# Re-spacing the DFT pieces of a spectral mixing and MLP kernel between its MLP steps

## The chip, the cores and the metric

The kernel runs on one core of a Trainium2 chip. The metric is the device time of one launch in microseconds (us); a time is the median of several launches. Every launch compared here counts as fast, that is, none was over 1.5% above the fastest launch of the same kernel.

TensorE (PE) does the matmuls and writes them to PSUM. VectorE (DVE) and ScalarE (ACT) move results out of PSUM. SyncE (SP) issues most DMAs. GpSimd (POOL) issues the loads of filters, weights and `x`; those of `x` change it from float32 to float16 on the way.

## The reference, cut to what matters

```python
B, S, C, DFF = 8, 3008, 256, 2048
X = np.fft.rfft(x, axis=1)                       # x: (8, 3008, 256)
y = np.fft.irfft(X * (filt_r + 1j * filt_i), n=S, axis=1)
h = y.reshape(B * S, C) @ w_in                   # (24064, 2048)
s = np.sin(alpha * h)
out = (h + s * s / (alpha + 1e-9)) @ w_out       # (24064, 256)
```

## The kernel before

The two transforms of a batch are split by 3008 = 47 x 64 into three stages. Between the stages the data goes through DRAM, because each stage needs another dimension on the partitions.

- Stage 1 (matmuls `pa`) turns `x` tiles into `t1` tiles, which are stored to the DRAM tensor `d1` ("the d1 store", `d<-t` in the profile). The whole of `d1` is read back as eight `t2` transfers (`t<-d`).
- Stage 2 (`pb`, then a product with the filter on VectorE, then `pc`) turns `t2` into `g`, stored to `d2` (`d<-g`). `d2` is read back as four `t4` tiles (also `t<-d`).
- The last stage (`pd`) turns `t4` into `y`, the input of the MLP.

The MLP (`ph` hidden, `po` projection) is one stream of 49 chunks of 8 steps, 48 steps to a batch on average. Stage pieces of the following batches are put in between, each at a step that a plan gives. The parts that matter (cuts marked `# ...`):

```python
xpool = pool("xp", 4)                   # four x tiles: one batch
fps = pool("fps", 2, PSUM)              # two PSUM buffers for pa, pb, pc, pd

def load_x(b):                          # four loads on GpSimd's queue
    for ch in range(4):
        xt = xpool.tile([NR, 8, C], FP16, name=f"x_{b}_{ch}", tag="x")
        ins = nc.gpsimd.dma_start(out=xt, in_=...)
        if b == 1:
            after(ins, marks["t4"])     # a true wait on a landing
        # ...

def stage1(u):
    ch, half = divmod(u, 2)
    if u == 0:
        st["x"] = load_x(b)
    # ... two pa matmuls from x tile ch, evicted to t1; with half == 1:
    #     nc.sync.dma_start(out=d1_rows[...], in_=st["t1"])
    # ... with u == 7: the eight t2 loads, each waiting for all of d1

def stage2(u):
    # ... with u < 12: pb, xf = copy(pb), two products; with u > 0: pc of u - 1, eviction to g

plan = {1: [-45 + i for i in range(8)],
        2: [-29 + 14 * i / 13 for i in range(13)],
        3: [-10, -9] + [-7 + 2 * i for i in range(14)]}
# ... a piece of batch b stands at step 48 * b + plan[stage][i];
#     batch 1 has 8 + i for stage 1 and 23 + i for stage 2

for k in range(len(chunks) + 1):
    for j in range(8):                  # one step
        hidden(k, 2 * j); hidden(k, 2 * j + 1)
        while pending and pending[0][0] <= step:
            pending.pop(0)[2]()         # the stage pieces due
        # ... project(k - 1, ...)
        step += 1
```

`behind(a, b)` orders two instructions at build time; `after(a, b)` makes `a` wait for `b` at run time. Anything else waits only for its data and its buffers.

## Time and profile before

| | before |
|---|---|
| time, median of the first 3 launches | 840.69 us (840.57 to 841.27) |
| span of the profiled launch | 837.2 us, granted TensorE clock 0.988 |
| first hidden matmul | 54.3 us |
| stalls of TensorE over 60 ns, all / after 80 us | 48.1 / 12.9 us |
| last stage-1 matmul to first stage-2 matmul, batches 2 to 7 | 16.7 us |

The head of the page: busy microseconds, and their share of the span, for each engine.

```profile
span 837.2 us, 16122 instructions
...
PE 799.8 (96%) x5793; PEld 544.2 (65%) x5793; DVE 628.1 (75%) x1119; ACT 613.0 (73%) x1200; POOL 28.3 (3%) x55
```

PE is busy 96% of the span. A busy record does not show a full rate, so the fourth table row comes from the start times of the single matmuls in the trace: the floor of a matmul with N columns is N / 2.4 GHz plus 2.5 ns (the Trainium skill's figure that the prediction names), and what lies above it, to the next matmul's start, is its stall. (The few float32 matmuls at the start are charged four times N; the trace has 853 ns for one with N = 512.) Back to back the trace shows 109 ns for N = 256 and 216 ns for N = 512, which is that floor.

The waits view of TensorE: who waited for whom, microseconds in total, times, longest.

```profile
PE pd L219 <- DMA t<-d: 10.9, 2, 9.3
PE pa L157 <- DMA x<-in_x_dram: 6.3, 1, 6.3
PE po L369 <- DVE w L337: 2.6, 1, 2.6
PE pb L180 <- DMA t<-d: 1.5, 1, 1.5
```

Nearly all of this is the start.

The timeline around the end of batch 2's stage 1: start, duration (microseconds), engine, line, operation, out<-in, count. A DMA line shows its issue, not its transfer. The transfer's end shows in who waits for it: all eight t2 loads wait for the last d1 store.

```profile
175.84 0.52 POOL L118 DMA_DIRECT2D x<-in_x_dram  x1 [4.21 <-PE pa L157]
...
177.53 4.81 SPq L161 DMA_DIRECT2D d<-t  x2
...
179.68 0.60 PE L157 MATMUL pa<-x,wf_t 94*96 94x512 f16 x2
...
180.57 0.52 POOL L118 DMA_DIRECT2D x<-in_x_dram  x1 [4.22 <-PE pa L157]
...
187.89 5.32 SPq L169 DMA_DIRECT2D t<-d  x8
...
196.60 0.38 PE L180 MATMUL pb<-t,d_t 128*128 128x256 f16 x2
```

Read it from top to bottom. Each x load of batch 3 goes out when a stage-1 matmul of batch 2 lets go of its buffer, so x loads and d1 stores run side by side. The last d1 store, issued at 182.0 us by the trace, lands at 187.8; the t2 loads follow at once. The first pair lands at 192.1 and is needed at 196.6: there are 4.5 us to spare. Not every batch has so much: batch 3's pair lands 1.8 us before its `pb`, batch 5's 2.2 us.

One more place, the timeline inside batch 2's dense stage 2:

```profile
201.89 0.75 DVE L187 TENSOR_TENSOR p<-xf,filt 128x512 f16<-128x512 f16 x2
...
202.56 0.68 DVE L137 CAST g<-pc 128x512 f16<-128x512 f32 x1
...
202.90 0.38 PE L369 MATMUL po<-w,v 128*128 128x256 f16 x2
...
203.30 0.60 PE L199 MATMUL pc<-p,e_t 128*128 128x256 f16 x4
```

The second `po` starts at 203.01, and `pc` could start 0.11 us later. It starts at 203.30, just after VectorE's eviction of the `pc` before it ended (202.56 + 0.68 = 203.24) and gave back one of the two `fps` buffers. After 80 us there are 24 such stalls before `pc`, 4.6 us.

### The profile page before, as it was taken

What the parts mean: (1) busy time and instruction counts of PE and PEld (TensorE: products, weight loads), DVE (VectorE), ACT (ScalarE), POOL (GpSimd) and SP (SyncE); (2) the same over time, 40 slices, a digit from 0 to 9 for tenths busy, and PEclk for the clock granted to TensorE, in tenths of its full rate; (3) what the DMA queues carried; (4) which work ended last, traced back from release to release, by engine and by line L of the source; (5) the groups of instructions that cost most, each with busy time, mean ns of one, the idle gap of its engine ahead of it and who ended that gap; (6) DMA issues with size and microseconds to landing.
All of it is one profiled execution on the core that took longest, in us unless ns stands there. A gap on an engine that the chain in (4) does not pass through costs nothing.

```text
span 837.2 us, 16122 instructions
## 1 busy us (share of the span) xinstructions
PE 799.8 (96%) x5793; PEld 544.2 (65%) x5793; DVE 628.1 (75%) x1119; ACT 613.0 (73%) x1200; POOL 28.3 (3%) x55
## 2 busy tenths in 40 slices
PE   5758999999999999999999999999999999999996
PEld 2425676667776677666776677666777677666674
DVE  3658886778877788777877788777877778777772
ACT  4536886787868787787877777777877878677763
POOL 3210000000000000000000000000000000000000
PEclk9969999999999999999999999999999999999999
DMA  9985835185344744266242763447443353421111
GB/s 220 218 255 117 200 89 130 51 174 116 82 135 81 171 99 109 75 141 153 65 130 60 165 137 82 115 91 171 92 96 94 97 113 83 115 58 38 38 40 45
DMA packets 93495, 94.98 MB, mean 113 GB/s; under 512 B 8084, under 2 KB 82852, under 8 KB 93416
## 3 DMA queue, kind: packets, MB, share of 16 engines
q1 hardware_dynamic: 84784, 75.02, 34.5%
q0 software_dynamic: 6704, 18.09, 12.5%
q10 hardware_dynamic: 1928, 0.86, 0.5%
q8 instruction: 45, 0.74, 0.3%
q14 instruction: 34, 0.28, 0.1%
HBM read 58.02 MB, written 49.81 MB: 129 GB/s over the span
## 4 chain that ended last, share of the span: by engine, by line
PE 83%; DMA 7%; ACT 4%; issue 3%; DVE 2%; POOL 0%; SPq 0%; ACTq 0%; DVEq 0%; POOLq 0%
PE po L369 36%; PE ph L354 35%; PE pc L199 4%; PE pa L157 3%; ACT cos L357 2%; PE pd L219 2%; PE pb L180 2%; DMA t<-d 1%; DMA w_out<-in_moe_w_out_dram 1%; DMA d<-g 1%; DMA d_t<-d_tbl 1%; DVE p L187 1%; DMA x<-in_x_dram 1%; DMA filt<-in_filt_i_dram 1%; ACT t L135 1%
## 5 line engine op out<-in xcount | busy, mean ns | idle before, releaser
L358 DVE SCALAR_TENSOR_TENSOR v<-cos,ph 128x512 f16<-128x512 f32 (+1 forms) x768 | 484.0, 672 | 164.0 <-ACT cos L357 163.5
L357 ACT ACTIVATE cos<-ph 128x512 f32<-128x512 f32 (+1 forms) x768 | 411.6, 589 | 153.9 <-PE ph L354 152.5
L369 PE MATMUL po<-w,v 128*128 128x256 f16 x3008 | 400.9, 273 | 2.6 <-DVE w L337 2.6
L354 PE MATMUL ph<-y,w 128*128 128x512 f16 (+1 forms) x1536 | 391.5, 377 | 0.2 <-ACT y L135 0.2
L369 PEld LDWEIGHTS <-v 128*128 128x128 f16 x3008 | 289.0, 98 | 80.9 <-issue 8.7
L354 PEld LDWEIGHTS <-w 128*128 128x128 f16 x1536 | 150.4, 98 | 101.0 <-issue 4.6
L187 DVE TENSOR_TENSOR p<-xf,filt 128x512 f16<-128x512 f16 x192 | 72.1, 419 | 4.9 <-ACT xf L183 4.5
L375 ACT COPY o<-po 128x512 f32<-128x512 f32 x96 | 55.6, 579 | 17.7 <-PE po L369 15.5
L135 ACT CAST t<-pa 96x512 f16<-96x512 f32 x89 | 51.0, 589 | 19.0 <-PE pa L157 18.9
L183 ACT CAST xf<-pb 128x512 f16<-128x512 f32 x96 | 57.0, 595 | 8.1 <-PE pb L180 5.5
L219 PEld LDWEIGHTS <-t 96*128 96x128 f16 x512 | 36.3, 100 | 39.8 <-DMA t<-d 11.8
L199 PE MATMUL pc<-p,e_t 128*128 128x256 f16 x384 | 59.7, 275 | 2.6 <-DVE p L187 1.5
L157 PE MATMUL pa<-x,wf_t 94*96 94x512 f16 x128 | 47.2, 408 | 10.1 <-DMA x<-in_x_dram 6.3
L219 PE MATMUL pd<-wi_t,t 96*128 96x94 f16 x512 | 43.4, 208 | 11.1 <-DMA t<-d 10.9
L135 ACT CAST y<-pd 128x376 f16<-128x376 f32 x82 | 39.1, 479 | 12.5 <-PE pd L219 12.5
L199 PEld LDWEIGHTS <-e_t 128*128 128x128 f16 x384 | 37.6, 99 | 15.6 <-issue 7.1
L180 PE MATMUL pb<-t,d_t 128*128 128x256 f16 x192 | 38.2, 283 | 2.5 <-DMA t<-d 1.5
L135 ACT CAST g<-pc 128x512 f16<-128x512 f32 x64 | 38.7, 605 | 1.6 <-PE pc L199 1.6
L137 DVE CAST t<-pa 96x512 f16<-96x512 f32 x39 | 26.6, 683 | 15.8 <-PE pa L157 15.8
L180 PEld LDWEIGHTS <-d_t 128*128 128x128 f16 x192 | 18.9, 101 | 23.8 <-issue 4.6
L118 POOL DMA_DIRECT2D x<-in_x_dram x32 | 16.7, 524 | 502.8 <-PE pa L157 490.5
L157 PEld LDWEIGHTS <-wf_t 94*96 94x96 f16 x128 | 16.6, 129 | 19.6 <-issue 9.9
(28 smaller groups left out, 94.3 us busy)
## 6 DMA issues: line engine op xcount, KB each, us to landing
d<-t SPq DMA_DIRECT2D x32, 384.0 KB
d<-g SPq DMA_DIRECT2D x64, 192.0 KB
t<-d SPq DMA_DIRECT2D x32, 384.0 KB
x<-in_x_dram POOLq DMA_DIRECT2D x32, 376.0 KB, 6.9
t<-d SPq DMA_DIRECT2D x60, 192.0 KB
out_dram<-o SPq DMA_DIRECT2D x72, 94.0 KB
w_in<-in_moe_w_in_dram POOLq DMA_DIRECT2D x2, 1024.0 KB, 9.2
w_out<-in_moe_w_out_dram POOLq DMA_DIRECT2D x1, 2048.0 KB, 11.6
```

The lines of the kernel that those rows point to most:

```text
L135: marks["act"] = nc.scalar.copy(out=dst, in_=src)
L157: marks["pe"] = nc.tensor.matmul(out=ps[0:NK, :], lhsT=wf_t, rhs=st["x"][ch][:, n0:n0 + 2, :], start=True, stop=True)
L180: nc.tensor.matmul(out=ps[:, i, :], lhsT=d_t[:, s, :], rhs=st["t2"][s // 6][:, s % 6, :], start=True, stop=True)
L183: nc.scalar.copy(out=xf, in_=ps)
L187: marks["prod", u] = nc.vector.tensor_tensor(out=pt, in0=xf, in1=f_t[k][:, 2 * u:2 * u + 2, :], op=ALU.mult)
L199: nc.tensor.matmul(out=ps[:, i, :], lhsT=e_t[:, k, 2 * w + i, :], rhs=pr[k][:, i, :], start=(k == 0), stop=(k == 1))
L219: nc.tensor.matmul(out=psv[:, i, :], lhsT=st["t4"][:, 4 * half + i, cb * 128:cb * 128 + 128], rhs=wi_t, start=True, stop=True)
L354: nc.tensor.matmul(out=ps[:, 0:n], lhsT=w1[:, cb, jb * 128:jb * 128 + 128], rhs=y_cols[:, cb, c0:c0 + n], start=(cb == 0), stop=(cb == 1))
L357: nc.scalar.activation(out=cs[:, 0:n], in_=ps[:, 0:n], func=AFT.Sin, bias=float(np.pi / 2))
L358: marks["snake"] = nc.vector.scalar_tensor_tensor(out=v[k][:, jb, 0:n], in0=cs[:, 0:n], scalar=-1.0, in1=ps[:, 0:n], op0=ALU.add, op1=ALU. ...
L369: nc.tensor.matmul(out=pso[k][:, t % 2, :], lhsT=v[k][:, jb, 128 * t:128 * t + 128], rhs=w2[:, jb, :], start=(jb == 0), stop=(jb == 15))
L375: nc.scalar.copy(out=o[:, 0:nb, :], in_=pso[k][:, 0:nb, :])
```

## The change

The intent: spread stage 2 over 24 steps so that evictions keep up, move the last stage further into its own batch's MLP, put the x loads behind the t2 loads, and load each t4 tile one ahead. Stage 1 moves from -45 to -50, stage 2 from -29 to -36, and odd batches go four steps earlier still. That cuts the room between the last stage-1 piece and the first stage-2 piece from nine steps to seven. The core of the diff, long refactorings cut:

```diff
         def stage1(u):
-            if u == 0:
+            if u == 0 and b < 2:
                 st["x"] = load_x(b)
# ... stage2 is split into forward, product and inverse, same work
+        def load_t4(ch):
+            st["t4", ch] = t4pool.tile([NK, 8, C], FP16, name=f"t4_{b}_{ch}", tag="t4")
+            marks["t4"] = nc.sync.dma_start(out=st["t4", ch], in_=d2_rows[:, 8 * ch:8 * ch + 8, :])
         def stage3(u):
             if rest == 0:
-                # ... load t4 tile ch
+                for c in ([0, 1] if ch == 0 else [ch + 1] if ch < 3 else []):
+                    load_t4(c)
# ...
+        if b >= 2:
+            pieces.append((0, lambda: st.update(x=load_x(b))))
# ... the sign of the imaginary part moves from e_t to the filter tile
-    plan = {1: [-45 + i for i in range(8)],
-            2: [-29 + 14 * i / 13 for i in range(13)],
-            3: [-10, -9] + [-7 + 2 * i for i in range(14)]}
+    def at_step(b, stage, i):
+        if b == 1 and stage < 3:
+            return 6 + i if stage == 1 else 21 + i
+        return 48 * b - 4 * (b % 2) + (-72 if stage == 0 else -50 + i if stage == 1
+                                       else -36 + 24 * i / 12 if stage == 2
+                                       else -6 + i if i < 4 else -1 + 2 * (i - 4))
```

A side effect: `w_out`'s load waits for `marks["t4"]`, the last t4 load emitted so far. That was tile 0 of batch 0 and is now tile 1.

More of the change, by code (lines that the diff above doesn't have):

```diff
@@ L171, in stage1, with forward @@
                     st["t2"].append(t2)
+        def forward(u):
+            ps = (ops if b == 0 else fps).tile([128, 2, C], FP32, name=f"pb_{b}_{u}",
+                                               tag="o" if b == 0 else "f")
+            for i in range(2):
+                s = 2 * u + i
+                nc.tensor.matmul(out=ps[:, i, :], lhsT=d_t[:, s, :],
+                                 rhs=st["t2"][s // 6][:, s % 6, :], start=True, stop=True)
+            xf = xfpool.tile([128, 2, C], FP16, name=f"xf_{b}_{u}", tag="xf")
+            nc.scalar.copy(out=xf, in_=ps)
+            st["xf", u] = xf
@@ new lines, in product, with inverse @@
+        def product(k, u):
+            pt = ppool.tile([128, 2, C], FP16, name=f"p_{b}_{u}_{k}", tag="p")
+            marks["prod", u] = nc.vector.tensor_tensor(out=pt, in0=st["xf", u],
+                                                       in1=f_t[k][:, 2 * u:2 * u + 2, :], op=ALU.mult)
+            return pt
+        def inverse(w):
+            pr = st.pop(("p", w))
+            if w % 3 == 0:
+                st["g"] = gpool.tile([128, 6, C], FP16, name=f"g_{b}_{w}", tag="g")
+            ps = fps.tile([128, 2, C], FP32, name=f"pc_{b}_{w}", tag="f")
+            for i in range(2):
+                for k, pt in enumerate(pr):
+                    nc.tensor.matmul(out=ps[:, i, :], lhsT=e_t[:, k, 2 * w + i, :],
+                                     rhs=pt[:, i, :], start=(k == 0), stop=(k == len(pr) - 1))
+            i0 = 2 * (w % 3)
+            evac(st["g"][:, i0:i0 + 2, :], ps, i0 != 2 if b == 0 else None)
+            if w % 3 == 2:
+                for p in range(2):
+                    a0 = p * NS + 6 * (w // 3)
+                    nc.sync.dma_start(out=d2[a0:a0 + 6, :, :].rearrange("s n c -> n s c"),
+                                      in_=st["g"][64 * p:64 * p + 64, :, :])
@@ L173, in stage2 @@
         def stage2(u):
             if u < 12:
-                ps = (ops if b == 0 else fps).tile([128, 2, C], FP32, name=f"pb_{b}_{u}",
-                                                   tag="o" if b == 0 else "f")
-                for i in range(2):
-                    s = 2 * u + i
-                    nc.tensor.matmul(out=ps[:, i, :], lhsT=d_t[:, s, :],
-                                     rhs=st["t2"][s // 6][:, s % 6, :], start=True, stop=True)
-                xf = xfpool.tile([128, 2, C], FP16, name=f"xf_{b}_{u}", tag="xf")
@@ L183, in stage2 @@
-                nc.scalar.copy(out=xf, in_=ps)
-                pr = []
-                for k in range(2):
-                    pt = ppool.tile([128, 2, C], FP16, name=f"p_{b}_{u}_{k}", tag="p")
-                    marks["prod", u] = nc.vector.tensor_tensor(out=pt, in0=xf, in1=f_t[k][:, 2 * u:2 * u + 2, :],
-                                                               op=ALU.mult)
-                    pr.append(pt)
-                st["p", u] = pr
-            if u > 0:
-                w = u - 1
-                pr = st.pop(("p", w))
-                if w % 3 == 0:
-                    st["g"] = gpool.tile([128, 6, C], FP16, name=f"g_{b}_{w}", tag="g")
-                ps = fps.tile([128, 2, C], FP32, name=f"pc_{b}_{w}", tag="f")
-                for i in range(2):
-                    for k in range(2):
-                        nc.tensor.matmul(out=ps[:, i, :], lhsT=e_t[:, k, 2 * w + i, :],
-                                         rhs=pr[k][:, i, :], start=(k == 0), stop=(k == 1))
-                i0 = 2 * (w % 3)
-                evac(st["g"][:, i0:i0 + 2, :], ps, i0 != 2 if b == 0 else None)
-                if w % 3 == 2:
-                    for p in range(2):
-                        a0 = p * NS + 6 * (w // 3)
-                        nc.sync.dma_start(out=d2[a0:a0 + 6, :, :].rearrange("s n c -> n s c"),
-                                          in_=st["g"][64 * p:64 * p + 64, :, :])
@@ L209, in stage3 @@
+                forward(u)
+                st["p", u] = [product(k, u) for k in range(2)]
+            if u > 0:
+                inverse(u - 1)
+        def load_t4(ch):
+            st["t4", ch] = t4pool.tile([NK, 8, C], FP16, name=f"t4_{b}_{ch}", tag="t4")
+            marks["t4"] = nc.sync.dma_start(out=st["t4", ch], in_=d2_rows[:, 8 * ch:8 * ch + 8, :])
         def stage3(u):
@@ L212, in stage3 @@
             if rest == 0:
-                t4 = t4pool.tile([NK, 8, C], FP16, name=f"t4_{b}_{ch}", tag="t4")
-                marks["t4"] = nc.sync.dma_start(out=t4, in_=d2_rows[:, 8 * ch:8 * ch + 8, :])
-                st["t4"] = t4
+                for c in ([0, 1] if ch == 0 else [ch + 1] if ch < 3 else []):
+                    load_t4(c)
             ps = fps.tile([128, 4, 128], FP32, name=f"pd_{b}_{u}", tag="f")
@@ L219, in stage3 @@
                 nc.tensor.matmul(out=psv[:, i, :],
-                                 lhsT=st["t4"][:, 4 * half + i, cb * 128:cb * 128 + 128],
+                                 lhsT=st["t4", ch][:, 4 * half + i, cb * 128:cb * 128 + 128],
                                  rhs=wi_t, start=True, stop=True)
@@ L266, in dup_filter @@
         gs = slice(6 * g, 6 * g + 6)
-        for k in range(2):
-            ins = nc.vector.tensor_copy(out=f_t[k][64:128, gs, :], in_=f_t[k][0:64, gs, :])
+        for ins in (nc.vector.tensor_copy(out=f_t[0][64:128, gs, :], in_=f_t[0][0:64, gs, :]),
+                    nc.vector.tensor_scalar(out=f_t[1][0:64, gs, :], in0=f_t[1][64:128, gs, :],
+                                            scalar1=-1.0, scalar2=None, op0=ALU.mult)):
             behind(ins, marks["prod", 3 * g - 2] if g else s1_dve)
@@ L275 @@
                 ins = nc.gpsimd.dma_start(
-                    out=f_t[k][32 * q:32 * q + 32, 6 * g:6 * g + 6, :],
+                    out=f_t[k][64 * k + 32 * q:64 * k + 32 * q + 32, 6 * g:6 * g + 6, :],
                     in_=bass.AP(tensor=filt.tensor, offset=filt.offset + off,
@@ L287 @@
         behind(nc.scalar.mul(e_t[:, 0, gs, :], pse, 0.125), s1_act)
-        nc.vector.tensor_copy(out=e_t[0:64, 1, gs, :], in_=e_t[64:128, 0, gs, :])
-        nc.vector.tensor_scalar(out=e_t[64:128, 1, gs, :], in0=e_t[0:64, 0, gs, :],
-                                scalar1=-1.0, scalar2=None, op0=ALU.mult)
+        for p in range(2):
+            nc.vector.tensor_scalar(out=e_t[64 * p:64 * p + 64, 1, gs, :],
+                                    in0=e_t[64 - 64 * p:128 - 64 * p, 0, gs, :],
+                                    scalar1=-1.0, scalar2=None, op0=ALU.mult)
     ones = cpool.tile([128, 128], FP32)
@@ L391, in store @@
             p += cnt
-    plan = {1: [-45 + i for i in range(8)],
-            2: [-29 + 14 * i / 13 for i in range(13)],
-            3: [-10, -9] + [-7 + 2 * i for i in range(14)]}
+    def at_step(b, stage, i):
[4 more added lines that the diff above has]
+                                       else -6 + i if i < 4 else -1 + 2 * (i - 4))
     pending = [(1 + i % 4 + 8 * (i // 4), 0, piece) for i, (_, piece) in enumerate(first[25:])]
     for b in range(1, B):
-        at = {1: 0, 2: 0, 3: 0}
+        at = {0: 0, 1: 0, 2: 0, 3: 0}
         for stage, piece in spectral(b):
-            at_step = 48 * b + plan[stage][at[stage]]
-            if b == 1 and stage < 3:
-                at_step = 8 + at[stage] if stage == 1 else 23 + at[stage]
+            pending.append((at_step(b, stage, at[stage]), b, piece))
             at[stage] += 1
-            pending.append((at_step, b, piece))
     pending.sort(key=lambda p: p[0])
```

## The prediction

> **What bounds the kernel now.** TensorE. The page gives PE 799.8 us of a 837.2 us span (96%), and the windows view 19.8 to 20.0 of nearly every 20 us from 80 us on. That proves little (the Trainium skill, "Perfetto Trace Analysis", opening note, calls matmul busy time a bad metric because matmuls are pipelined), so I took start-to-start times from the trace. Back to back, 128x256 projections start every 109 ns, 128x512 hidden matmuls every 216 ns. That agrees with the skill's "TensorE: Matmul & The Clock Gate", section "Wait — 56ns, not 53.3ns?": N / 2.4 GHz plus about 2.5 ns. Charging each matmul that floor, the matmuls after 80 us need 735 us and lose only 13 us to stalls over 60 ns. By what came after the stall: stage 1 (pa) 5.8 us in 29 stalls, the second stage's inverse (pc) 4.6 us in 24, the last stage (pd) 2.0 us, of which 1.78 us is one wait at 141 us for batch 1's t4. The remaining loss is the start: first hidden matmul at 54.3 us, and 2.65 us of waiting for w_out at 62 us. So at most 13 us, 1.5%, can be won.
>
> **What the change does.** Matmuls, evictions and bytes stay. The filter's sign moves from e_t to f_t: 421 ns against 423 ns, nothing.
> - Stage 2 over 24 steps rather than 14. The timeline at 200 to 214 us shows the stall: pc waits for one of two fps buffers, whose eviction (683 ns) stands on VectorE behind other work; about four 0.18 to 0.24 us stalls a batch. With a piece every second step VectorE has about 4.2 us for what it now does in 2.45. Gone: -4 us.
> - Batch 1 moves two steps earlier while its last stage stays at step 38: the 1.78 us wait goes: -1.8 us.
> - Stage 1 still fills both fps buffers, now with more last-stage pieces in the same steps for odd batches: +0.5 us.
> - From the last stage-1 matmul to the first stage-2 matmul, room falls from 9 steps (16.7 us: 179.9 to 196.6) to 7, about 13 us. The first t2 pair lands 11.3 to 15 us after that matmul (x loads run beside the d1 stores, which take 5 to 9 us). Stage 1's own matmuls release the x loads (the waits view), so they should not move. Batches 3 and 5 may wait 1.5 to 2 us each, some others less: +2 us. If the x loads do move behind the t2 loads: 0.
> - w_out's load now waits for t4 tile 1 rather than 0, starting 1 to 1.5 us later, where PE already waits: +1 us.
> - Room between stage 2 and the last stage stays six steps; t4 lands within 0.8 us of need: 0 to +1 us.
>
> **Sum.** 840.7 - 5.8 + 3.5 = about 838.4; the t2 waits are uncertain, so lower: 837.5 us, 8 in 10 between 833 and 841.5. Faster by over 2%: 0.01; within 2%: 0.98; slower by over 2%: 0.01.
>
> **What would show it.** The waits view: PE pd for t4 falls from 10.9 to about 9.3 us; PE pb for t2 grows by 0 to 4 us; w_out's wait grows from 2.6 to 3.6 us. Stage-2 windows show VectorE near 15 rather than 17 of 20 us, and short gaps before pc vanish.
>
> **What would make it wrong.** New DMA waits in every batch, another order on TensorE, or growing pa and pd stalls over PSUM buffers.

## More of the kernel before

The wait of `pb` for t2 is a single one, in batch 0. So before, no later batch waits for t2.

## The result

| | before | after |
|---|---|---|
| time, median of 4 launches | 840.92 us (840.57 to 841.27) | 863.18 us (860.80 to 867.80) |
| span of the profiled launch, granted clock | 837.2 us, 0.988 | 860.5 us, 0.980 |
| TensorE stalls over 60 ns, all / after 80 us | 48.1 / 12.9 us | 71.2 / 31.7 us |

The change made the kernel slower: the ratio is 1.0271, 95% interval 1.0227 to 1.0316. Ratios here are the mean time of one kernel's fast runs over that of the other's of the same rounds, so not quite the ratio of the medians quoted. The stalls grew by 23.1 us and the span by 23.3, so the stalls are the whole difference.

The page of after, and its waits view of TensorE:

```profile
span 860.5 us, 16111 instructions
...
PE 804.1 (93%) x5793; PEld 545.6 (63%) x5793; DVE 630.3 (73%) x1119; ACT 614.1 (71%) x1200; POOL 28.2 (3%) x55
```

```profile
PE pb L179 <- DMA t<-d: 16.4, 7, 3.8
PE pd L229 <- DMA t<-d: 11.4, 2, 9.2
PE pa L157 <- DMA x<-in_x_dram: 5.9, 1, 5.9
PE po L383 <- DVE w L351: 5.6, 1, 5.6
```

The wait of `pb` for t2 is now in seven batches rather than one; w_out's wait doubled. PE did the same 5793 matmuls.

The timeline of after, again at the end of batch 2's stage 1:

```profile
174.63 0.51 POOL L118 DMA_DIRECT2D x<-in_x_dram  x1 [4.22 <-PE po L383]
...
178.80 0.38 PE L157 MATMUL pa<-x,wf_t 94*96 94x512 f16 x1
...
179.47 0.51 POOL L118 DMA_DIRECT2D x<-in_x_dram  x1 [4.33 <-PE pa L157]
...
179.82 0.32 SPq L161 DMA_DIRECT2D d<-t  x1
...
188.87 5.28 SPq L169 DMA_DIRECT2D t<-d  x8
...
192.98 0.38 PE L179 MATMUL pb<-t,d_t 128*128 128x256 f16 x2 [1.89 <-DMA t<-d]
```

The x loads still go out beside the d1 stores, the last one 0.7 us after the last stage-1 matmul began, as before. Being emitted elsewhere in the program did not move them. The last d1 store takes 9.0 us (issued 179.8, landed 188.9 in the trace). The first t2 pair lands at 192.84, and `pb` starts at 192.98, with TensorE idle for 1.89 us ahead of it.

What follows a longer wait is in the timeline of after behind batch 3's wait:

```profile
278.94 1.04 PE L383 MATMUL po<-w,v 128*128 128x256 f16 x8
279.81 1.03 PE L368 MATMUL ph<-y,w 128*128 128x512 f16 x4
284.67 0.58 PE L179 MATMUL pb<-t,d_t 128*128 128x256 f16 x2 [3.83 <-DMA t<-d]
285.05 1.91 PE L383 MATMUL po<-w,v 128*128 128x256 f16 x8
286.76 1.91 PE L368 MATMUL ph<-y,w 128*128 128x512 f16 x4
```

The eight `po` and the four `ph` took 1.04 and 1.03 us ahead of the wait and take 1.91 us each after it. The clock that TensorE is granted has halved, and the wait of 3.8 us costs another 2.2 us. The Trainium skill, "TensorE: Matmul & The Clock Gate", Part 1, describes this: an idle TensorE falls to half clock and needs some microseconds of work to come back.

Where the 23 us went, from the matmul start times, stalls over 60 ns sorted by the matmul that came after the stall:

| us of stalls | before | after |
|---|---|---|
| up to 80 us (the start) | 35.2 | 39.5 |
| then: before pb (t2) | 0 | 15.2 |
| before po and ph (in after nearly all half clock) | 0.5 | 4.8 |
| before pd | 2.0 | 3.4 |
| before pa | 5.8 | 7.0 |
| before pc | 4.6 | 1.3 |
| sum | 48.1 | 71.2 |

### The profile page after: what moved, and what is told of

It is laid out like the page before. It is cut to its first block, busy times and chain, and to the rows that moved or that the text cites. A ratio compares the mean times of both kernels' runs of the same rounds, so it can differ in the third digit from the quotient of the medians.

```text
span 860.5 us, 16111 instructions
## 1 busy us (share of the span) xinstructions
PE 804.1 (93%) x5793; PEld 545.6 (63%) x5793; DVE 630.3 (73%) x1119; ACT 614.1 (71%) x1200; POOL 28.2 (3%) x55
## 3 DMA queue, kind: packets, MB, share of 16 engines
q0 software_dynamic: 6704, 18.09, 12.3%
## 4 chain that ended last, share of the span: by engine, by line
PE 73%; DMA 15%; ACT 4%; DVE 3%; issue 2%; SPq 1%; ACTq 0%; DVEq 0%; POOLq 0%
PE po L383 31%; PE ph L368 30%; DMA d<-t 7%; PE pc L198 5%; DMA t<-d 4%; PE pa L157 3%; PE pb L179 2%; DMA out_dram<-o 2%; ACT cos L371 2%; DMA w_out<-in_moe_w_out_dram 2%; PE pd L229 1%; DVE v L372 1%; ACT t L135 1%; SPq L169 1%; DVE t L137 1%
## 5 line engine op out<-in xcount | busy, mean ns | idle before, releaser
L187 DVE TENSOR_TENSOR p<-xf,filt 128x512 f16<-128x512 f16 x192 | 72.2, 420 | 16.6 <-ACT xf L182 16.5
L135 ACT CAST t<-pa 96x512 f16<-96x512 f32 x85 | 48.9, 590 | 25.0 <-PE pa L157 25.0
L229 PEld LDWEIGHTS <-t 96*128 96x128 f16 x512 | 36.4, 100 | 41.2 <-DMA t<-d 12.5
L229 PE MATMUL pd<-wi_t,t 96*128 96x94 f16 x512 | 43.2, 209 | 11.9 <-DMA t<-d 11.4
L135 ACT CAST y<-pd 128x376 f16<-128x376 f32 x86 | 41.2, 481 | 11.8 <-PE pd L229 11.8
L198 PEld LDWEIGHTS <-e_t 128*128 128x128 f16 x384 | 37.3, 98 | 12.5 <-issue 3.2
L137 DVE CAST t<-pa 96x512 f16<-96x512 f32 x43 | 29.4, 683 | 16.7 <-PE pa L157 16.5
L135 ACT CAST g<-pc 128x512 f16<-128x512 f32 x64 | 39.5, 617 | 1.4 <-PE pc L198 1.4
L118 POOL DMA_DIRECT2D x<-in_x_dram x32 | 16.6, 524 | 514.8 <-PE po L383 360.2
L157 PEld LDWEIGHTS <-wf_t 94*96 94x96 f16 x128 | 16.6, 130 | 18.4 <-issue 10.1
## 6 DMA issues: line engine op xcount, KB each, us to landing
w_out<-in_moe_w_out_dram POOLq DMA_DIRECT2D x1, 2048.0 KB, 14.4
```

The costliest lines, as they stand in the source:

```text
L135: marks["act"] = nc.scalar.copy(out=dst, in_=src)
L157: marks["pe"] = nc.tensor.matmul(out=ps[0:NK, :], lhsT=wf_t, rhs=st["x"][ch][:, n0:n0 + 2, :], start=True, stop=True)
L187: marks["prod", u] = nc.vector.tensor_tensor(out=pt, in0=st["xf", u], in1=f_t[k][:, 2 * u:2 * u + 2, :], op=ALU.mult)
L198: nc.tensor.matmul(out=ps[:, i, :], lhsT=e_t[:, k, 2 * w + i, :], rhs=pt[:, i, :], start=(k == 0), stop=(k == len(pr) - 1))
L229: nc.tensor.matmul(out=psv[:, i, :], lhsT=st["t4", ch][:, 4 * half + i, cb * 128:cb * 128 + 128], rhs=wi_t, start=True, stop=True)
```

## The experiments

The theory (A in the expectations): the x loads of the next batch run beside the d1 stores and stretch them, and the shortened room no longer hides that, so TensorE waits for t2 in each batch and then runs slowly for a while. Rivals: spreading stage 2 costs the time through buffers or eviction engines (B); the longer start is the larger part (C); the new place of the x loads in the program brought them onto the d1 stores (D). All kernels but `h1_half_x` gave correct results. Each run's time stands beside launches of the kernel before on the same chip in the same set: 840.3 us (first four), 840.13 us (second four), 840.75 us (last four).

| label | base and edit | median us | ratio to before (95%) |
|---|---|---|---|
| a1_x_behind_t2 | after, x loads wait for t2 | 842.56 | 1.0023 (1.0002 to 1.0043) |
| a2_gap9 | after, nine steps of room | 841.33 | 1.0014 (0.9983 to 1.0044) |
| a3_dense | after, stage 2 in 14 steps | 869.06 | 1.0339 (1.0321 to 1.0356) |
| a4_wout0 | after, w_out behind t4 tile 0 | 861.42 | 1.0254 (1.0225 to 1.0283) |
| a7_x_old_place | after, x loads emitted as before | 861.48 | 1.0246 (1.0219 to 1.0273) |
| b2_gap7 | before, seven steps of room | 845.01 | 1.0070 (1.0038 to 1.0102) |
| b3_gap7_x | b2_gap7, x loads wait for t2 | 841.26 | 1.0014 (1.0000 to 1.0027) |
| b1_x_behind_t2 | before, x loads wait for t2 | 839.76 | 0.9988 (0.9968 to 1.0007) |
| h1_half_x | after, half the bytes of x | 842.71 | 1.0022 (1.0005 to 1.0038) |
| h2_x_behind_d1 | after, x loads wait for d1 | 885.54 | 1.0527 (1.0481 to 1.0573) |
| a5_x_wout | a1 and a4 together | 838.33 | 0.9969 (0.9952 to 0.9986) |
| a6_best | a5, batch 1's stage 2 a step earlier | 837.36 | 0.9967 (0.9953 to 0.9980) |

For the theory's own quantities, this table has five kernels, batches 2 to 6 and, in brackets, batch 7, after which no x load follows. The times are from the trace: the last d1 store from issue to landing; the landing of the first t2 pair and the start of `pb`, both counted from the start of the last stage-1 matmul.

| us | before | after | a1_x_behind_t2 | h1_half_x | h2_x_behind_d1 |
|---|---|---|---|---|---|
| last d1 store | 5.5 to 8.7 (3.0) | 7.2 to 9.5 (3.3) | 3.0 to 3.1 (3.3) | 4.6 to 5.4 (3.4) | 3.0 to 3.3 (3.4) |
| first t2 pair landed | 11.9 to 14.9 (11.3) | 13.9 to 15.0 (8.9) | 8.2 to 9.3 (8.7) | 9.8 to 10.7 (9.0) | 15.9 to 16.7 (9.0) |
| pb started | 16.7 (16.7) | 14.0 to 15.1 (11.5) | 10.9 to 12.2 (11.5) | 10.9 to 12.2 (11.5) | 16.0 to 16.8 (11.5) |

Batch 7 is an experiment that every run contains: with no x load beside it, its d1 store takes 3.0 to 3.4 us in each kernel, and no `pb` waits.

### a1_x_behind_t2: the intent made true

```diff
             if b == 1:
                 after(ins, marks["t4"])
+            if b >= 2:
+                after(ins, marks["t2", 3])
```

> The changed kernel with one true wait added: from batch 2 on each x load waits for the landing of the last t2 load of the batch before. Theory A (x loads of the next batch run beside the d1 stores and double their time, and the cut room of about 11.5 to 12 us no longer hides it): the last d1 store lands in 3 to 4.5 us rather than 8 to 9.5, the TensorE wait of pb for t2 falls from 16.4 us to under 3, the half-clock stretches after it vanish, time 842 to 846 us. Rival B (the spreading of stage 2 and its overlap with the last stage cost the time, by PSUM buffers or eviction engines): time stays at 859 to 866 us.

Measured: 842.56 us. The waits view of TensorE, and below it the timeline at the end of batch 2's stage 1:

```profile
PE pd L231 <- DMA t<-d: 11.3, 2, 8.8
...
PE po L385 <- DVE w L353: 2.8, 1, 2.8
...
PE pb L181 <- DMA t<-d: 1.4, 1, 1.4
```

```profile
173.89 0.38 PE L159 MATMUL pa<-x,wf_t 94*96 94x512 f16 x1
...
174.91 0.32 SPq L163 DMA_DIRECT2D d<-t  x1
...
177.89 5.96 SPq L171 DMA_DIRECT2D t<-d  x8
...
186.01 0.38 PE L181 MATMUL pb<-t,d_t 128*128 128x256 f16 x2
...
188.93 1.53 POOL L118 DMA_DIRECT2D x<-in_x_dram  x3 [85.58 <-DMA out_dram<-o]
```

The d1 store is done 3.0 us after its issue, `pb` has no wait left but batch 0's, and the x loads go out only after stage 2 has begun (the view names an output store as what ended their wait; the last t2 load landed at 188.4 in the trace). This one dependency gives back some 20 of the 22 us. Stage 2 is still spread over 24 steps here, so rival B falls.

### a2_gap9: more room, x loads where they were

```diff
-  -72 if stage == 0 else -50 + i if stage == 1
+  -74 if stage == 0 else -52 + i if stage == 1
```

> The changed kernel with stage 1 (and the x loads' place) two steps earlier from batch 2 on, so that nine steps lie between stage 1 and stage 2 as before; x loads still beside the d1 stores. Theory A: the room grows by about 3.5 us, the waits of 2 to 4 us mostly vanish (pb for t2 from 16.4 to 1.5 to 4 us, batch 1's 1.6 stays), time 844 to 849 us, with d1 stores still at 8 to 9 us. Rival B: no gain, 859 to 866 us.

Measured: 841.33 us, better than the 844 to 849 expected. The last d1 stores of batches 2 to 6 still take 7.9 to 9.1 us, but `pb`'s stalls after 80 us are 2.1 us in two batches, and the half-clock stretches after them are gone. Either of two cures is enough, fast d1 stores or room for slow ones; it takes both ills to lose the 20 us.

### a3_dense and a4_wout0: the rivals

```diff
# a3_dense
-  else -36 + 24 * i / 12 if stage == 2
+  else -36 + 14 * i / 13 if stage == 2
# a4_wout0
+            if b == 0 and ch == 0:
+                marks["t4 0"] = marks["t4"]
-    after(nc.gpsimd.dma_start(out=w_out32, ...), marks["t4"])
+    after(nc.gpsimd.dma_start(out=w_out32, ...), marks["t4 0"])
```

> The changed kernel with stage 2 packed into 14 steps again from batch 2 on, starting at the same step. Theory A: the waits for t2 stay (14 to 18 us), and the short pc stalls of about 0.2 us come back (plus 2 to 4 us): 861 to 869 us. Rival B (spreading is what costs): back to 840 to 848 us.

> The changed kernel with w_out's load waiting for t4 tile 0 of batch 0 as before, not tile 1. Theory A with a start term of 3 us: the wait of po for w2 falls from 5.6 to about 3 us, time 858 to 862 us, t2 waits unchanged. Rival C (the lost start and the slow clock after it are the larger part): 850 us or less.

Packing stage 2 again made it worse, 869.06 us: the t2 stalls stay (17.3 us), the pc stalls return (1.3 to 3.3 us), and the last stage's stalls grow to 8.9 us, probably because the dense stage 2 now stands among last-stage pieces of the batch before, for which the two PSUM buffers must serve too. Spreading is a gain, not the loss. a4_wout0 got 861.42 us: w_out's landing came at 64.0 rather than 68.5 us, the t2 waits stayed (13.5 us of stalls before `pb`). Rival C falls.

### a7_x_old_place: does the place in the program matter?

```diff
-            if u == 0 and b < 2:
+            if u == 0:
                 st["x"] = load_x(b)
-        if b >= 2:
-            pieces.append((0, lambda: st.update(x=load_x(b))))
```

> The changed kernel with the x loads emitted where they were before, as part of the first stage-1 piece. Theory A (the place of emission is inert, because what holds an x load is only the release of its buffer by stage 1's matmuls): the four loads still go out 13 us before to 0.7 us after the last stage-1 matmul of the batch before, t2 waits 14 to 18 us, time 859 to 866 us. Rival D (the new place is what brought the x loads onto the d1 stores): time falls to 841 to 848 us.

Measured: 861.48 us. The four x loads of batch 3 go out 13.5, 8.9 and 4.2 us before and 0.7 us after batch 2's last stage-1 matmul, to 0.1 us the same as in after. The place is inert, rival D falls, and so does the change's claim that it put the x loads behind the t2 loads. A warning for reading waits: GpSimd's waits view of after puts 360.2 us of the x loads' waits down to `po` and 146.2 to `pa`, where before had 490.5 on `pa`. That looks as if the loads had moved to another releaser. Their issue times say that they had not.

### b2_gap7, b3_gap7_x and b1_x_behind_t2: the same on the kernel before

```diff
# b2_gap7, and b3_gap7_x with a1's edit besides
-            2: [-29 + 14 * i / 13 for i in range(13)],
+            2: [-31 + 14 * i / 13 for i in range(13)],
# b1_x_behind_t2: a1's edit alone
```

> The kernel before with stage 2 of batches 2 to 7 starting two steps earlier and nothing else, so seven steps of room rather than nine, x loads beside the d1 stores as ever. Theory A: room falls from 16.7 to about 13.3 us against t2 landings of 12 to 15 us; PE waits for t2 in batches 3 and 5 and little elsewhere, 3 to 6 us in all, time 842 to 848 us. Rival B (room is not it): time within 1 us of before.

> As b2_gap7, with each x load from batch 2 on waiting for the last t2 load of the batch before. Theory A: d1 stores land in 3 to 4 us, no wait for t2 with seven steps of room, time 839 to 842 us. Rival B: same as b2_gap7, whatever that is.

> The kernel before with only its x loads from batch 2 on held behind the last t2 load of the batch before. Theory A: the d1 stores fall from 5 to 9 us to about 3 us, but with 16.7 us of room nothing waited for them, so the time is unchanged: 839 to 842 us. Rival: the d1 stores' slowness already cost time before: under 838 us.

With seven steps of room, the kernel before loses 5 us (845.01). The profiled launch is the slowest of the four (851.03); it has 5.9 us of stalls before `pb`, in batches 3, 5 and slightly 6, and some 5 us more than before ahead of `pd`, `po` and `ph`, much of it at half clock. With true waits on the x loads this loss goes (841.26; no stall before `pb` after 80 us). With nine steps the faster d1 stores (3.0 to 3.5 us) bring nothing that can be told from noise (839.76, interval across 1): nothing waited for them.

So room alone costs 5 us on the kernel before and the same cut in steps costs 20 on the changed one. Two sources of that difference can be measured. First, seven steps are 13.1 us in b2_gap7 and b3_gap7_x, where no wait stretches them, but only 12.1 to 12.2 (even batches) and 10.9 to 11.1 us (odd) in a1. Second, the d1 stores beside x loads took 5.2 to 5.9 us in b2_gap7's batches 2 and 4, and 9.0 and 8.8 in after's. The shorter steps hold less work. From the last stage-1 matmul to the first `pb`, the trace of b2_gap7 has 56 `po`, 28 `ph` and 16 `pd` matmuls; a1's has 49 or 50 `po` and 12 `pd` in even batches, 40 `po` and 12 `pd` in batches 3 and 5, with 27 or 28 `ph`. The floors of these add up to 13.0, 12.1 to 12.2 and 10.9 to 11.1 us, which is the whole room. The 40 `po` have their reason in the plan: odd batches, moved four steps, now have this room where the projections of the short last chunk of the batch pair run (384 columns, six half tiles over eight steps rather than eight). Batch 1 keeps its eight steps, yet its room too falls, from 14.1 to 12.5 us (58 `po` and 32 `ph` become 51 and 28). Why the even batches' d1 stores became slower is open. In batches 2 and 4 of after they are issued 0.35 and 0.5 us after an x load, where before and b2_gap7 have 1.45 us, but no run isolated this.

### h1_half_x and h2_x_behind_d1: what about an x load hurts?

```diff
# h1_half_x (wrong results on purpose)
-  xt = xpool.tile([NR, 8, C], FP16, ...)
+  xt = xpool.tile([NR, 8 if b < 2 else 4, C], FP16, ...)
#  ... the load's pattern likewise, and stage 1 reads n0 % 4 for n0
# h2_x_behind_d1
+            if b >= 2:
+                after(ins, marks["d1"])
```

> The changed kernel with x loads of half the bytes from batch 2 on (each tile's second half is computed from its first: wrong results on purpose). It asks what in the x load holds the d1 store back. If it is the bytes in flight: the last d1 store falls from 8 to 9.5 us to about 5.5 to 6.5 us, the t2 pair lands 10 to 11.5 us after the last stage-1 matmul, waits of pb for t2 fall from 16 to under 4 us, time 842 to 848 us. If it is a cost per load that does not depend on bytes: d1 stores stay over 7.5 us and the time over 855 us.

> The changed kernel with each x load from batch 2 on waiting for the landing of the last d1 store of the batch before, so that x loads run beside the t2 loads instead. Theory A: d1 stores take 3 us; the t2 pair, now the one beside the x loads, lands later than the 8 to 9 us of a1_x_behind_t2 but before 12; waits of pb for t2 0 to 6 us in all, time 842 to 850 us. If x loads hurt any transfer equally (4 to 6 us): the t2 pair lands at 13 us or later and the time stays over 855 us.

Half the bytes brought the d1 stores to 4.6 to 5.4 us, below the 5.5 to 6.5 expected, and removed all t2 stalls after 80 us (842.71 us). So the harm goes with the bytes of the x loads, not with their number, nor with that of their packets: the pages of after and h1_half_x both count 6704 packets on GpSimd's queue, with 18.09 and 13.47 MB. The Trainium skill, "Trainium Kernel Development and Optimization", Key Constraints, says that DMAs from the SP, ACT and POOL queues run on the same 16 DMA engines and interleave; this run fits that, without showing the engines.

h2_x_behind_d1 was a miss for my figure: 885.54 us rather than 842 to 850, the worst kernel of all. With the d1 stores free (3.0 to 3.3 us), all four x loads start at once beside the t2 loads. Its waits view shows what that does:

```profile
PE pb L181 <- DMA t<-d: 30.3, 7, 6.2
```

The first t2 pair lands 15.9 to 16.7 us after the last stage-1 matmul. The first transfer of batch 2's pair landed 3.0 us after its issue; its packets ran first (from 191 to 192 us the trace has 381 on SyncE's queue and 8 of the x loads). The second took 11.3 us, with four x loads issued around it. While they run together, from 195 to 200 us, SyncE's queue moves 312 packets and 0.16 MB, GpSimd's 265 packets and 0.93 MB (`prof h2_x_behind_d1 --dma --window 195:200`): about as many packets, but the data packets of t2 have 512 bytes and those of x 4096. Alone, from 179 to 183 us of a1_x_behind_t2, SyncE's queue moves 0.82 MB in 4 us. This would fit turns taken packet by packet, in which the transfer with small packets loses; no run varied the packet size. "Behind the d1 stores" and "behind the t2 loads" sound alike and lie 43 us apart.

### a5_x_wout and a6_best: keeping the good parts

a5_x_wout has a1's and a4's edits; a6_best has these and

```diff
-            return 6 + i if stage == 1 else 21 + i
+            return 6 + i if stage == 1 else 20 + i
```

> a1_x_behind_t2 with w_out waiting for t4 tile 0, that is a6_best without batch 1's earlier stage 2. If w_out's place is worth 1 us: 840 to 842.5 us; batch 1's wait for t4 stays at 2.3 to 3 us with the half-clock microseconds after it. If w_out's place is worth nothing beyond run-to-run spread: same as a1_x_behind_t2, 842 to 843.5 us.

> The changed kernel with x loads truly behind the t2 loads, w_out waiting for t4 tile 0 as before, and batch 1's stage 2 one step earlier. Theory A: no waits for t2 beyond the start, w_out's wait 2.5 to 3.5 us, batch 1's wait for t4 falls from 2.6 to about 1 us, pc stalls stay gone: 836 to 840 us, that is up to 0.5 per cent faster than before. If theory A missed a second cost of the new plan: above 841 us.

Both are a little faster than the kernel before, by 0.3%, with intervals that end below 1: 838.33 us (ratio 0.9969) and 837.36 us (0.9967). They were run in different sets, and the two ratios don't tell them apart. a5 gained more over a1 than expected (838.33 for 840 to 842.5); in its profiled launch batch 1's wait for t4 is still 2.6 us, but no half clock follows it; in a1's it cost 1.3 us. a6_best's time is as expected; its w_out wait, 4.8 us, is not (2.5 to 3.5). In a6_best's waits of `pd` for t4 only batch 0's is left:

```profile
PE pd L233 <- DMA t<-d: 8.6, 1, 8.6
...
PE po L387 <- DVE w L355: 4.8, 1, 4.8
...
PE pb L181 <- DMA t<-d: 1.9, 2, 1.8
```

After 80 us its stalls are 9.2 us against 12.9 before: `pc` 1.5 (4.6), `pd` 0.5 (2.0), `pa` 7.0 (5.8). That is the gain that the spreading was meant for, less what stage 1 lost; its start is 2.5 us longer in that launch (37.7 against 35.2).

## Why the prediction was wrong

The prediction said 837.5 us, 833 to 841.5, with 0.98 for "within 2%". Measured were 863.18 us and slower by 2.7%. It was wrong in its number and its class. Point by point:

- TensorE is the bound and at most 13 us can be won after 80 us: nothing measured contradicts it. The best version found wins 3.7 us there.
- The pc stalls go, -4 us: right in kind, measured -3.3 us (4.6 to 1.3). VectorE's busy time in the stage-2 windows, though, fell from 17.4 to 16.6 of 20 us on average, not to 15.
- Stage 1's stalls, +0.5 us: measured +1.2 us.
- Batch 1's wait for t4 goes, -1.8 us: wrong. The stall was 1.78 us and became 2.34 us. Two steps earlier gave less than it seems: from the last `pc` to the need for t4 there are 10.6 us rather than 9.3, and d2 lands 5.6 us after that `pc` rather than 6.3, which is 2.1 us won. But the trace shows the first t4 load issued 1.6 us after the landing of d2, behind five output stores on SyncE's queue, where before it was 0.1 us, and taking 5.7 us rather than 4.6: 2.6 us lost. The longer start is not the reason: a1_x_behind_t2 has the start of before and a wait of 2.6 us. One step earlier for stage 2, together with a5's edits, removed the wait in a6_best: no output store came between, and the load took 3.4 us.
- w_out, +1 us: under-sized. The load did start 1.3 us later (54.1 for 52.8), as predicted, but took 14.4 us rather than 11.6, and why is open. Its wait grew by 3.0 us in the profiled launch (2.6 to 5.6), and the start's stalls by 4.3. The landing varied from run to run: 66.2 to 69.8 us over the seven profiled launches with tile 1's wait, 64.0 to 65.7 over the seven with tile 0's.
- t4 of the later batches, 0 to +1 us: right. The stalls before `pd` other than batch 1's wait went from 0.2 to 1.1 us, part of that at half clock.
- The x loads do not move, as stage 1's matmuls release them: right, and a7_x_old_place shows it.
- **The step that failed** is this term: "Batches 3 and 5 may wait 1.5 to 2 us each, some others less: +2 us." The mechanism was right, the size was not: it measured 15.2 us of stalls before `pb`, in all of batches 1 to 6, and half clock after those of batches 3 and 5 added 3.3 us before `po` and `ph` (another 1.4 us followed batch 1's wait for t4). The prediction had named "New DMA waits in every batch" as what would make it wrong, and that is what came. Three inputs of the term were wrong. The room was put at 13 us by scaling 16.7 us with steps; unstalled it is 12.2 in even and 11.0 in odd batches (a1_x_behind_t2), because the steps there hold fewer matmuls. The landings of 11.3 to 15 us were carried over from before, as if x loads and d1 stores would meet as they did; after has 13.9 to 15.0 us in every batch that an x load follows. And the clock after a wait was not in the sum at all, though the start of the trace showed it: hidden matmuls start 427 ns apart at 55 us, where 216 is the full rate.

Taking landing less room with the measured values, 14.0 - 12.2 (batches 2, 4, 6) and 14.7 - 11.0 (3 and 5), gives 1.8 us for an even and 3.7 for an odd batch, which is about what the trace has (1.9 and 3.8 on average). A range as narrow as 8.5 us, with a term that takes the difference of two numbers of 13 us each in six batches, was too sure: an error of 1 us in either moves it by 6. And the prediction lowered its sum from 838.4 to 837.5 because the t2 waits were uncertain, for the case that the x loads move, although it had just argued that they would not; the uncertainty lay on the other side.

## What to carry to other kernels

A slow transfer that nobody waits for is invisible in a profile of busy time and waits; before shortening the distance between a producer and its consumer, read the landing of what lies between, batch by batch, and subtract. Where a load is emitted in the program doesn't say when it runs: here GpSimd issued it as soon as its buffer was free, in after and a7_x_old_place alike, so an order of transfers needs a true wait, and a wait on the wrong transfer (h2_x_behind_d1) can be worse than none. An idle gap on TensorE costs more than its length once it halves the clock: here 3.8 us cost another 2.2.

## What the Trainium skill lacked or had wrong

- "TensorE: Matmul & The Clock Gate", Part 1, puts the fall to half clock after at least one idle window of about 3.4 us. In the 14 profiled launches here, no stall after 80 us of under 2.02 us halved the clock for more than a single matmul, 13 of 21 stalls between 2.02 and 3.00 us did, and all 14 of 3.04 us or more. So shorter waits than one window can cost, and not always. Where it happened, the half rate cost 1.2 to 2.7 us in the 8 us after.
- "DMA: Bandwidth & Descriptors", section "Anatomy of one DMA — SWDGE (gpsimd) path", gives a transfer about 2.0 us plus bytes / 436 GB/s. It is stated for GpSimd's queue, but holds for a d1 store on SyncE's queue too when that is alone: 393 KB make an estimate of 2.9 us, and 3.0 was measured. It gives no time for two transfers in flight. The same sum over both (393 KB, and the 770 KB that an x load reads) would be an estimate of 4.7 us, and d1 stores beside x loads took 7.2 to 9.5 us in the changed kernel (the estimate leaves out the x load before, which is in flight too: issued at 174.6, landed at 182.5 us in batch 2 of after); with half the x bytes the estimate is 3.8 us, and 4.6 to 5.4 was measured.
- "Trainium Kernel Development and Optimization", Key Constraints, says that DMAs of all queues interleave on the same 16 engines. It gives no figure for what that does to latency, nor does "DMA: Bandwidth & Descriptors", section "Queues, rings and completion order": here the loads nobody was in a hurry for held back the ones on the way to TensorE by up to 6.5 us (d1 store, 9.5 for 3.0) and 8 us (second t2 transfer of batch 2 in h2_x_behind_d1, 11.3 us after 3.0 for the first).
